# Top-32 attention and a squared-ReLU FFN on one core: the late loop's scores, mark passes and dense pieces in another order, and the pairing of four more steps on GpSimd

## Chip, cores and metric

One core of a Trainium2 chip runs the whole kernel. The metric is the device time of one execution in microseconds (us), the median of several runs. The engines are TensorE (PE), VectorE (DVE), ScalarE (ACT), GpSimd (POOL) and SyncE (SP), which issues most of the transfers. Each works through its own queue in order and waits where an operand or a buffer is not ready.

## What is computed

Eight batches of eight heads, 576 positions, head size 64. Each row of scores keeps its 32 largest values; their softmax weighs v. The eight heads of a position side by side give x (4608 x 512), which goes through a dense layer with a squared ReLU.

```python
scores = scale * np.matmul(q, k.transpose(0, 1, 3, 2))
kth = np.partition(scores, -top_k, axis=-1)[..., -top_k:-top_k + 1]
scores = np.where(scores >= kth, scores, -1000000000.0)
attn = np.exp(scores - np.max(scores, axis=-1, keepdims=True))
attn = attn / (np.sum(attn, axis=-1, keepdims=True) + 1e-09)
x = np.matmul(attn, v)                     # then (4608, 512)
h = np.maximum(x @ w_in, 0.0)              # 512 -> 2048
return h * h @ w_out                       # 2048 -> 512
```

## The kernel before

**Steps.** The attention is cut into 144 steps, numbered 0 to 143 (`U = 144`). A step holds two tiles of 128 rows by 576 scores. Steps 0 to 124 run in the first loop (L702), steps 125 (`Z = U - 19`) to 141 in the **late loop** (L798), the last two behind it. The change lies in the late loop and in `split`, which both loops use. All operations are pinned: each engine works in the order in which the program writes them.

**The life of a step u**, spread over several turns of the loop:

- `ahead` calls `scores` (L206): PE multiplies q and k (L213) into two PSUM tiles, `sc_b` for the second half of the columns and `sc_a` for the first, and ACT copies them into a buffer `s` in SBUF (L219, first `sc_b`, then `sc_a`). There is one `sc_a` and one `sc_b` for all steps. In turn u of the late loop this is done for step u + 3.
- `split` (L237, for step u + 2) and `join` (L260) pair the columns off: `cat` gets the pairwise maxima and minima of the two halves, and again of the halves of these. `split` has two forms. In the **old form** DVE does three operations of 128 x 288 (L253, L254, L256). In the **lent form** DVE does one maximum of 128 x 576 (L251), and the minima come from GpSimd: `mins` (L272) adds the two halves (L278), and `catch_up` (L267), a turn later, subtracts the maxima from the sum (L270). In the lent form the far half of the maxima lies in SBUF, and `bring` (L232) has PE move it, by a product with the identity (L235), into a free part of `sc_b` called `far`, where `join` reads it. `bring(u + 2)` comes behind the copy of `sc_b` for step u + 3, since both use that bank. Where a step is also **joint**, the minima of `join` go to GpSimd as well (a larger addition and one more subtraction), and `join` is one DVE operation (L263) instead of two.
- `topk` (L292) searches the 32 largest in four rounds on DVE: two MAX8 (L302) and, but for the last round, two MATCH_REPLACE8 (L306) each. ACT makes a small tile `low` from the maximum (L345).
- `below` (L352) is a **mark pass**: ACT marks the scores under the 32nd largest of one tile (L354), so two per step. `expo` (L361) is ACT's exponential of both tiles (L363), `mask` (L357) GpSimd's addition that takes the marked weights out (L359), `turn` (L400) a transposing transfer on SP's queue (L402), `products` (L683) PE's products of weights and v (L429), `invert` DVE's reciprocal of the sums (L434), and `place` (L449) ACT's scaled copies of the result into `x_tok` (L457).

**Dense pieces.** Once x of 128 tokens is complete, SP transposes it and the FFN's work on it is put into two lists. An **up piece** is eight products by w_in (L531) into one of two PSUM tiles named `gen`; later ACT takes the ReLU (L537) into a buffer `rl`, and the square follows on GpSimd (L545) or on ACT (L542). A **down piece** is four products by w_out (L559); every fourth is followed by an output copy on ACT (L566) and a store. `piece` (L582) first calls `flush`, which writes what ACT still owes for earlier pieces, and then takes one up or down piece in turn; `idle_piece` (L575) fills PE with products nobody reads.

**The planner.** `owe` adds up estimated work for GpSimd and ACT in `debt`, which each turn lowers (L58). `split` lends if GpSimd's debt is low; the square goes to ACT where GpSimd's debt is high and ACT's is not (L540). A change in one place can thus move a square in another.

**One turn of the late loop** before the change, shortened to the lines that matter here:

```python
below(u - 1, 0)
below(u - 1, 1)
...
split(u + 2)
topk(u, (0,))
...
mins(u + 2)
weights(u - 1)      # mask and turn
...
ahead(u + 3)
topk(u, (1,))
piece()
bring(u + 2)
products(u - 2)
topk(u, (2, 3))
join(u + 2)
...
expo(u)
```

Behind these stand `place(u - 2)` and two or three more pieces (L850).

Of the kernel before, what the change touches and what calls it, by code (L numbers as in the profile page):

```python
# [22 lines left out]
def kernel(  # L23
# [22 lines left out]
    def pin(ins):  # L46
        tc.keep_in_program_order(ins)
        return ins

    debt = {"G": 0.0, "A": 0.0}  # L50

    def owe(**more):
        for e, t in more.items():
            debt[e] += t
# [3 lines left out]
    def pass_step(more=0.0):  # L58
        for e in debt:
            debt[e] = max(0.0, debt[e] - {"G": 5.76, "A": 6.0}[e] - more)  # L60
# [134 lines left out]
    U = len(steps)  # L195
    Z, DEEP = U - 19, 9
# [39 lines left out]

    def split(u):  # L237
        d = st[u]
        lend = (2 < u < U - 20 and debt["G"] < 4.9) or Z < u < U - 5
        d["joint"] = lend and DEEP + 5 <= u < U - 6 and debt["G"] < (4.9 if u < Z + 2 else 5.5) - 1.22  # L240
        if d["joint"]:
            owe(G=1.36)
        cat = d["cat"] = scp.tile([128, 2, S], f32, name="cat", bufs=3)
        tops = d["tops"]
        one, two = sc[0][:, :, 0:HALF], d["s"][:, :, 1, :]
        tt = nc.vector.tensor_tensor
        if lend:
            owe(G=1.22)
            d["lent"] = True
            quarters = [z.rearrange("p x (j n) -> p x j n", j=2) for z in (one, two)]  # L250
            pin(tt(tops, *quarters, op=ALU.max))  # L251
        else:
            pin(tt(far, one[:, :, QUAR:HALF], two[:, :, QUAR:HALF], op=ALU.max))  # L253
            pin(tt(tops[:, :, 0, :], one[:, :, 0:QUAR], two[:, :, 0:QUAR], op=ALU.max))  # L254
        if not lend:
            pin(tt(cat[:, :, HALF + QUAR:S], one[:, :, QUAR:HALF], two[:, :, QUAR:HALF], op=ALU.min))  # L256
        if "rest" in d:
            d.pop("rest")()
# [75 lines left out]
    def sums_checked(by, lo, hi):  # L334
        pin(by.tensor_scalar(flags[:, 2, lo:hi], shares[:, lo:hi], scalar1=2.0 ** -12, scalar2=0.0, op0=ALU.is_ge, op1=ALU.is_equal))
# [13 lines left out]
    def pairwise(z):  # L349
        return z.rearrange("p (j n) -> p j n", j=2)  # L350

    def below(u, x):  # L352
        d = st[u]
        pin(nc.scalar.activation(pairwise(marks[u % 2][:, x, :]), d["s"][:, x], AF.Relu, bias=d["m"][3][:, x, 7:8], scale=-1.0))  # L354
        follow()
# [17 lines left out]
    def follow():  # L373
        while later:
            later.pop(0)()
# [7 lines left out]
    def flush():  # L383
        while late:
            late.pop(0)()
# [196 lines left out]
    def piece():  # L582
        flush()
        turn_of[0] ^= 1
        for q_ in ((ups, downs), (downs, ups))[turn_of[0]]:
            if q_:
                q_.pop(0)()
                return True
        return False
# [90 lines left out]
    def ok(w):  # L680
        return 0 <= w < U

    def products(w):  # L683
        if ok(w):
            for x in range(2):
                weigh(w, x)
# [8 lines left out]
    def ahead(w):  # L695
        if w < U:
            for i, c, a in steps[w]:
                while coming <= i or (coming == i + 1 and soon):
                    prepare(u)
            scores(w)  # L700
# [89 lines left out]
    def weights(w):  # L790
        mask(w)
        turn(w)

    def move():
        while moves:
            moves.pop(0)(u)

    for u in range(Z, U - 2):  # L798
        now[0] = u
        pass_step(0.3)  # L800
        owe(A=3.86, G=2.92)
        below(u - 1, 0)
        below(u - 1, 1)
        move()
        split(u + 2)
        topk(u, (0,))
        if u == Z:
            products(u - 3)
            invert_two(u - 4)
            place(u - 5)  # L810
            place(u - 4)
        if checks:
            note()
        mins(u + 2)
        if u == U - 8:
            sums_checked(nc.gpsimd, 0, OLD)
        weights(u - 1)
        square()
        hold["squares"] = False
        for go in ripe.pop(u, ()):  # L820
            go()
        ahead(u + 3)
        topk(u, (1,))
        if not piece():
            idle_piece()
        bring(u + 2)
        products(u - 2)
        if u < U - 4:
            topk(u, (2, 3))
        else:  # L830
            topk(u, (2,), lambda: invert(u - 2))
            topk(u, (3,))
        join(u + 2)
        if u == Z:
            invert(u - 3)
        if u < U - 4:
            invert(u - 2)
        if u == U - 4:
            piece()
        flush()  # L840
        expo(u)
        flush()
        if u == Z:
            place(u - 3)
        place(u - 2)
        turn_x(u)
        hold["squares"] = True
        for _ in range(2 if u == U - 19 else 1):
            prepare(u)
        for n in range(3 if u >= U - 12 and u != U - 4 else 2):  # L850
            if not piece() and n == 0:
                idle_piece()

# [10 lines left out]
    u = U - 2  # L864
# [72 lines left out]
    u = U - 1  # L937
# [190 lines left out]
```

## Time and profile before

| | |
|---|---|
| median of 3 runs | 842.77 us (842.25 to 844.38) |
| the profiled execution's own time | 843.64 us |
| its span, first to last recorded instruction | 841.8 us |
| mean granted clock of TensorE, share of full speed | 0.994 |
| instructions | 19913 |

The page of the profile lists for each engine its busy time and share of the span. A timeline lists one engine's instructions with start and duration in us; instructions that follow each other overlap a little, so what one costs its queue is read from start to start. The number in square brackets is idle time ahead of an instruction, with what ended it. The waits add such idle time up by what waited and what released it, and the chain of waits is followed back from the last instruction. All times of the trace count from the start of the span. Turn 125 of the late loop starts near 714 us on ACT, and one turn there takes about 6 us.

### The profile page before, as it was taken

What the parts mean: (1) busy time and instruction counts of PE and PEld (TensorE: products, weight loads), DVE (VectorE), ACT (ScalarE), POOL (GpSimd) and SP (SyncE); (2) the same over time, 40 slices, a digit from 0 to 9 for tenths busy, and PEclk for the clock granted to TensorE, in tenths of its full rate; (3) what the DMA queues carried; (4) which work ended last, traced back from release to release, by engine and by line L of the source; (5) the groups of instructions that cost most, each with busy time, mean ns of one, the idle gap of its engine ahead of it and who ended that gap; (6) DMA issues with size and microseconds to landing.
All of it is one profiled execution on the core that took longest, in us unless ns stands there. A gap on an engine that the chain in (4) does not pass through costs nothing.

```text
span 841.8 us, 19913 instructions
## 1 busy us (share of the span) xinstructions
PE 710.4 (84%) x6061; PEld 446.6 (53%) x6062; DVE 816.4 (97%) x3411; ACT 791.5 (94%) x1513; POOL 785.0 (93%) x638
## 2 busy tenths in 40 slices
PE   8898987788888879788788888788888888989986
PEld 4554545455545545455555554455555554656554
DVE  5999999999999999999999999999999999999995
ACT  4897999999999999999999999999999999999983
POOL 3788999999999999999999999999999999999771
PEclk9999999999999999999999999999999999999999
DMA  4796786654546556445565455555566557433442
GB/s 112 163 216 158 193 178 112 111 118 101 118 105 104 117 111 130 97 103 109 114 124 110 104 111 124 124 111 109 118 104 124 118 104 152 79 76 64 94 84 55
DMA packets 300883, 98.06 MB, mean 116 GB/s; under 512 B 284768, under 2 KB 293216, under 8 KB 300768
## 3 DMA queue, kind: packets, MB, share of 16 engines
q1 hardware_dynamic: 299424, 96.28, 56.1%
q8 instruction: 50, 0.82, 0.4%
q14 instruction: 65, 0.53, 0.2%
q10 hardware_dynamic: 1344, 0.43, 0.2%
HBM read 36.70 MB, written 9.44 MB: 55 GB/s over the span
## 4 chain that ended last, share of the span: by engine, by line
DVE 53%; issue 15%; POOL 13%; ACT 11%; PE 7%; DVEq 0%; ACTq 0%; POOLq 0%
DVE m L302 23%; DVE cat L306 15%; DVE s L251 7%; POOL cat L270 7%; DVE cat L263 5%; POOL cat L278 5%; ACT s L219 3%; ACT h L542 2%; PE sc_b L235 2%; ACT rl L537 1%; ACT marks_b L354 1%; ACT marks_a L354 1%; ACT w_two_a L363 1%; PE sc_b L213 1%; PE dn_ps L578 1%
## 5 line engine op out<-in xcount | busy, mean ns | idle before, releaser
L302 DVE MAX8 m<-cat 128x8 f32<-128x100 f32 (+3 forms) x1152 | 428.7, 414 | 0.2
L278 POOL TENSOR_TENSOR cat<-s 128x864 int32<-128x864 int32 (+2 forms) x144 | 265.0, 1840 | 5.9 <-DVE cat L263 3.5
L306 DVE MATCH_REPLACE8 cat<-m,cat 128x100 f32<-128x100 f32 (+2 forms) x864 | 252.7, 300 | 0.1
L270 POOL TENSOR_TENSOR cat<-cat,s 128x576 int32<-128x576 int32 (+1 forms) x144 | 196.3, 1363 | 3.3 <-DVE s L251 1.8
L213 PE MATMUL sc_b<-qkT 64*128 64x288 f32 (+1 forms) x640 | 117.4, 447 | 55.3 <-DVE cat L263 49.2
L235 PE MATMUL sc_b<-s,id_f 128*128 128x144 f32 x536 | 98.3, 306 | 57.4 <-ACT s L219 56.5
L559 PE MATMUL dn_ps<-w_out,h 128*128 128x512 bf16 x560 | 143.9, 382 | 1.3 <-POOL h L545 0.7
L531 PE MATMUL gen<-xT,w_in 128*128 128x256 bf16 (+1 forms) x1088 | 128.6, 263 | 1.9 <-ACT rl L537 1.1
L235 PEld LDWEIGHTS sc_b<-s,id_f 128*128 128x128 f32 x536 | 75.0, 190 | 101.0 <-ACT s L219 97.4
L531 PEld LDWEIGHTS <-w_in 128*128 128x128 bf16 x1344 | 110.2, 98 | 32.3 <-issue 19.7
L354 ACT ACTIVATE marks_a<-s,m 128x576 bf16<-128x576 f32 x144 | 124.2, 871 | 0.4 <-POOL w_two_c L359 0.2
L354 ACT ACTIVATE marks_b<-s,m 128x576 bf16<-128x576 f32 x142 | 118.5, 847 | 0.0
L219 ACT ACTIVATE s<-sc_b 128x576 f32<-128x576 f32 x144 | 103.7, 720 | 15.5 <-PE sc_b L213 8.2
L213 PE MATMUL sc_a<-qkT 64*128 64x288 f32 (+1 forms) x640 | 111.5, 430 | 0.4 <-DVE s L251 0.3
L219 ACT ACTIVATE s<-sc_a 128x576 f32<-128x576 f32 x144 | 104.8, 728 | 5.5 <-PE sc_a L213 3.7
L251 DVE TENSOR_TENSOR s<-sc_a,s 128x576 f32<-128x576 f32 x134 | 100.2, 748 | 0.0
L537 ACT ACTIVATE rl<-gen 128x512 f32<-128x512 f32 x140 | 96.3, 692 | 0.5 <-PE gen L531 0.5
L213 PEld LDWEIGHTS sc_b<-qkT 64*128 64x128 f32 (+1 forms) x640 | 47.6, 175 | 85.5 <-DVE cat L263 64.9
L270 POOL TENSOR_TENSOR cat<-cat 128x288 int32<-128x288 int32 x113 | 89.2, 789 | 0.9 <-DVE shares L434 0.9
L542 ACT ACTIVATE h<-rl 128x512 bf16<-128x512 f32 x123 | 89.2, 729 | 0.0
L559 PEld LDWEIGHTS <-h 128*128 128x128 bf16 x560 | 47.8, 98 | 68.4 <-issue 31.9
L263 DVE TENSOR_TENSOR cat<-sc_b,s 128x288 f32<-128x288 f32 x175 | 75.0, 444 | 5.8 <-PE sc_b L235 5.8
(137 smaller groups left out, 1190.5 us busy)
## 6 DMA issues: line engine op xcount, KB each, us to landing
v_raw<-in_v_dram SPq DMA_DIRECT2D x31, 256.0 KB, 3.1
out_dram<-wide SPq DMA_DIRECT2D x31, 256.0 KB, 2.9
q_raw<-in_q_dram SPq DMA_DIRECT2D x30, 256.0 KB, 3.6
k_raw<-in_k_dram SPq DMA_DIRECT2D x30, 256.0 KB, 3.6
h<-in_moe_w_in_dram SPq DMA_DIRECT2D x8, 512.0 KB, 5.1
h<-in_moe_w_out_dram SPq DMA_DIRECT2D x8, 512.0 KB, 4.7
q_raw<-in_q_dram SPq DMA_DIRECT2D x32, 32.0 KB, 3.1
v_raw<-in_v_dram SPq DMA_DIRECT2D x32, 32.0 KB, 2.7
```

What stands on the lines that cost most here:

```text
L213: pin(nc.tensor.matmul(out=sc[j][r if rest else slice(0, 128), x, 0:HALF], lhsT=qkT[r, 0, c * 128:min(S, (c + 1) * 128)], rhs=qkT[r, 1, j ...
L219: pin(nc.scalar.activation(s[:, :, j, :], sc[j][:, :, 0:HALF], AF.Copy))
L235: pin(nc.tensor.matmul(out=far[:, x, :], lhsT=id_f[:, :], rhs=st[w]["tops"][:, x, 1, :], start=True, stop=True))
L251: pin(tt(tops, *quarters, op=ALU.max))
L263: pin(nc.vector.tensor_tensor(d["cat"][:, :, lo:lo + QUAR], far, d["tops"][:, :, 0, :], op=op))
L270: pin(nc.gpsimd.tensor_tensor(at, at, top, op=ALU.subtract))
L278: pin(nc.gpsimd.tensor_tensor(cat[:, :, QUAR + lo:QUAR + hi], both[:, :, 0, lo:hi], both[:, :, 1, lo:hi], op=ALU.add))
L302: pin(nc.vector.max(out=m[r][:, x, :], in_=cat[:, x, at]))
L306: pin(nc.vector.match_replace(out=cat[:, x, at], in_to_replace=m[r][:, x, :], in_values=cat[:, x, at], imm_value=NEG))
L354: pin(nc.scalar.activation(pairwise(marks[u % 2][:, x, :]), d["s"][:, x], AF.Relu, bias=d["m"][3][:, x, 7:8], scale=-1.0))
L531: pin(nc.tensor.matmul(out=hp[:, n * n_rows:(n + 1) * n_rows], lhsT=w_in[:, kh, (f0 + n) * 128:(f0 + n + 1) * 128], rhs=xt(kh), start=(kh ...
L559: pin(nc.tensor.matmul(out=op[:, :], lhsT=held["h2"][:, f, c * 128:(c + 1) * 128], rhs=w_out[:, f, :], start=(f == 0), stop=(f == NF - 1)))
```

## The change

Four edits, in two functions:

1. `split` lends under another condition. Steps 124, 125, 139 and 140 now take the lent form (124 and 125 are also joint); before they took the old one.
2. The second mark pass and `move` (transposes of x that PE does) stand behind `ahead(u + 3)` instead of ahead of `split`.
3. `ahead(u + 3)` stands ahead of `weights`, `square` and the pieces that come ripe, instead of behind them. With edit 2 ACT's two copies of scores lie between the two mark passes.
4. One dense piece is done behind `products(u - 2)`, and one fewer at the end of the turn.

```diff
--- before.py
+++ after.py
@@ -236,7 +236,7 @@
 
     def split(u):
         d = st[u]
-        lend = (2 < u < U - 20 and debt["G"] < 4.9) or Z < u < U - 5
+        lend = 2 < u < U - 3 and (debt["G"] < 4.9 or u > Z)
         d["joint"] = lend and DEEP + 5 <= u < U - 6 and debt["G"] < (4.9 if u < Z + 2 else 5.5) - 1.22
         if d["joint"]:
             owe(G=1.36)
@@ -800,8 +800,6 @@
         pass_step(0.3)
         owe(A=3.86, G=2.92)
         below(u - 1, 0)
-        below(u - 1, 1)
-        move()
         split(u + 2)
         topk(u, (0,))
         if u == Z:
@@ -814,17 +812,20 @@
         mins(u + 2)
         if u == U - 8:
             sums_checked(nc.gpsimd, 0, OLD)
+        ahead(u + 3)
+        below(u - 1, 1)
+        move()
         weights(u - 1)
         square()
         hold["squares"] = False
         for go in ripe.pop(u, ()):
             go()
-        ahead(u + 3)
         topk(u, (1,))
         if not piece():
             idle_piece()
         bring(u + 2)
         products(u - 2)
+        piece()
         if u < U - 4:
             topk(u, (2, 3))
         else:
@@ -847,7 +848,7 @@
         hold["squares"] = True
         for _ in range(2 if u == U - 19 else 1):
             prepare(u)
-        for n in range(3 if u >= U - 12 and u != U - 4 else 2):
+        for n in range(2 if u >= U - 12 and u != U - 4 else 1):
             if not piece() and n == 0:
                 idle_piece()
```

ScalarE's queue in a turn of the middle of the late loop, before: `marks_a` is what the mark passes write, `s` the copied scores, `rl` the ReLU of an up piece, `gen` its PSUM tile, `h2` its square, `x_tok` the placed result.

```order
L354 ACTIVATE marks_a_117<-s_9643,m_9874 128x576
L219 ACTIVATE s_9981<-sc_b_123 128x2x288
L219 ACTIVATE s_9981<-sc_a_122 128x2x288
L345 ACTIVATE low_9990<-neg_9988 128x1
L537 ACTIVATE rl_9992<-gen_9948 128x512
L537 ACTIVATE rl_10023<-gen_9994 128x512
L363 ACTIVATE w_two_b_104<-s_9715,low_9990 128x2x576
L542 ACTIVATE h2_9901<-rl_9992 128x512
L542 ACTIVATE h2_9901<-rl_10023 128x512
L457 ACTIVATE x_tok_9091<-av_ps_121,shares_120 128x64 x2
L537 ACTIVATE rl_10040<-gen_10031 128x512
L354 ACTIVATE marks_b_118<-s_9715,m_9874 128x576 x2
```

And with the change, the same turn:

```order
L354 ACTIVATE marks_a_117<-s_9640,m_9873 128x576
L219 ACTIVATE s_9977<-sc_b_123 128x2x288
L219 ACTIVATE s_9977<-sc_a_122 128x2x288
L354 ACTIVATE marks_a_117<-s_9640,m_9873 128x576
L345 ACTIVATE low_9990<-neg_9988 128x1
L537 ACTIVATE rl_9992<-gen_9949 128x512
L537 ACTIVATE rl_10015<-gen_9994 128x512
L537 ACTIVATE rl_10034<-gen_10017 128x512
L363 ACTIVATE w_two_b_104<-s_9714,low_9990 128x2x576
L542 ACTIVATE h2_9901<-rl_9992 128x512
L542 ACTIVATE h2_9901<-rl_10015 128x512
L457 ACTIVATE x_tok_9091<-av_ps_121,shares_120 128x64 x2
```

The first mark pass is still ahead of the two copies and the second one is behind them; three ReLUs stand ahead of the exponential, where there were two and a third one behind the placing.

GpSimd's queue where step 124 is split (`cat_9563`) and then step 125 (`cat_9635` before, `cat_9634` with the change), before:

```order
L278 TENSOR_TENSOR cat_9563<-s_9482 128x2x144
L545 TENSOR_TENSOR h2_9097<-rl_9605 128x512
L359 TENSOR_TENSOR w_two_b_104<-w_two_b_104,marks_b_118 128x2x288
L163 CAST vau_a_97<-v_raw_115 128x10x64
L270 TENSOR_TENSOR cat_9563<-cat_9563,s_9482 128x2x144
L278 TENSOR_TENSOR cat_9635<-s_9571 128x2x144
L359 TENSOR_TENSOR w_two_c_105<-w_two_c_105,marks_a_117 128x2x288
```

And with the change:

```order
L278 TENSOR_TENSOR cat_9563<-s_9482 128x2x432
L359 TENSOR_TENSOR w_two_b_104<-w_two_b_104,marks_b_118 128x2x288
L163 CAST vau_a_97<-v_raw_115 128x10x64
L270 TENSOR_TENSOR cat_9563<-cat_9563 128x2x144
L270 TENSOR_TENSOR cat_9563<-cat_9563,s_9482 128x2x288
L278 TENSOR_TENSOR cat_9634<-s_9569 128x2x432
L359 TENSOR_TENSOR w_two_c_105<-w_two_c_105,marks_a_117 128x2x288
```

The additions (L278) of these steps grow from 128 x 2 x 144 to 128 x 2 x 432, the subtraction (L270) of step 124 becomes two, and the square (L545) has left GpSimd's queue for ACT's.

## Rows read from the trace of the kernel before

**Rows 1.** The page, first part: busy us (share of the span) and instructions of each engine.

```profile
PE 710.4 (84%) x6061; PEld 446.6 (53%) x6062; DVE 816.4 (97%) x3411; ACT 791.5 (94%) x1513; POOL 785.0 (93%) x638
```

**Rows 2.** Busy time by stretch: window, length, busy (instructions) per engine, PEclk, DMA share, GB/s.

```profile
760.00:780.00 20.00, 19.62 (x212) 13.78 (x212) 18.50 (x82) 20.00 (x43) 18.90 (x15) 1.00 0.48 80
800.00:820.00 20.00, 16.62 (x183) 10.67 (x180) 19.87 (x87) 16.67 (x33) 14.71 (x15) 1.00 0.40 81
```

**Rows 3.** The waits from 700 to 842 us: waiter, releaser, total us, count, median.

```profile
DVE cat L263 <- PE sc_b L235: 4.0, 6, 1.1
```

**Rows 4.** The chain of waits from 690 to 842 us: start, us, instruction.

```profile
732.92 0.55 ACT s L219
733.51 0.77 PE sc_b L235 x4
734.38 0.46 DVE cat L263
```

**Rows 5.** ScalarE in order of time, 717 to 736: start, us, instruction [idle before <-releaser].

```profile
717.88 0.93 ACT L457 ACTIVATE x_tok<-av_ps,shares 128x64 bf16<-128x64 f32 x4 [0.21 <-DVE shares L434]
...
731.36 1.56 ACT L354 ACTIVATE marks_b<-s,m 128x576 bf16<-128x576 f32 x2
732.69 0.77 ACT L219 ACTIVATE s<-sc_b 128x576 f32<-128x576 f32 x1
733.22 0.78 ACT L219 ACTIVATE s<-sc_a 128x576 f32<-128x576 f32 x1
733.75 0.34 ACT L345 ACTIVATE low<-neg 128x1 f32<-128x1 f32 x1
733.85 1.23 ACT L537 ACTIVATE rl<-gen 128x512 f32<-128x512 f32 x2
734.80 1.41 ACT L363 ACTIVATE w_two_c<-s,low 128x1152 bf16<-128x1152 f32 x1
```

**Rows 6.** VectorE in order of time, 700 to 708 us.

```profile
700.06 0.47 DVE L253 TENSOR_TENSOR sc_b<-sc_a,s 128x288 f32<-128x288 f32 x1
...
701.16 0.42 DVE L302 MAX8 m<-cat 128x8 f32<-128x100 f32 x2
...
705.68 0.81 DVE L263 TENSOR_TENSOR cat<-sc_b,s 128x288 f32<-128x288 f32 x2
706.40 0.75 DVE L251 TENSOR_TENSOR s<-sc_a,s 128x576 f32<-128x576 f32 x1
707.06 0.42 DVE L302 MAX8 m<-cat 128x8 f32<-128x100 f32 x2
```

**Rows 7.** GpSimd in order of time, 698 to 718 us.

```profile
698.44 0.78 POOL L270 TENSOR_TENSOR cat<-cat 128x288 int32<-128x288 int32 x1
699.19 1.40 POOL L270 TENSOR_TENSOR cat<-cat,s 128x576 int32<-128x576 int32 x1
700.56 0.79 POOL L278 TENSOR_TENSOR cat<-s 128x288 int32<-128x288 int32 x1
701.32 1.03 POOL L545 TENSOR_TENSOR h<-rl 128x512 bf16<-128x512 f32 x1
...
706.14 1.41 POOL L359 TENSOR_TENSOR w_two_c<-w_two_c,marks_a 128x576 int32<-128x576 int32 x1 [0.25 <-ACT w_two_c L363]
...
708.25 2.02 POOL L278 TENSOR_TENSOR cat<-s 128x864 int32<-128x864 int32 x1
711.16 1.42 POOL L359 TENSOR_TENSOR w_two_a<-w_two_a,marks_b 128x576 int32<-128x576 int32 x1 [0.88 <-ACT w_two_a L363]
...
716.62 1.42 POOL L359 TENSOR_TENSOR w_two_b<-w_two_b,marks_a 128x576 int32<-128x576 int32 x1
```

**Rows 8.** TensorE in order of time, 721 to 736 us.

```profile
721.96 0.48 PE L429 MATMUL av_ps<-vau_c,wT 128*128 128x65 bf16 x10 [0.22 <-DMA wT<-w_two_b]
...
734.11 0.47 PE L429 MATMUL av_ps<-vau_e,wT 128*128 128x65 bf16 x10
734.63 1.03 PE L531 MATMUL gen<-xT,w_in 128*128 128x256 bf16 x8
```

## The prediction

> **What bounds the kernel now.** I read five views in this order. The busy line of the page [rows 1] has VectorE (DVE) at 97%, with ScalarE (ACT), GpSimd (POOL) and TensorE (PE) not far below; it cannot tell which of them holds up the late loop, where the change lies. The busy time by stretch [rows 2] can: from 760 to 780 us ACT is busy all 20.00 us and DVE only 18.50, while from 800 to 820 DVE has 19.87 and ACT 16.67. So ACT bounds the first part of the late loop and DVE its end. The waits [rows 3] name what DVE misses: six times, 4.0 us in all, `join` (L263) waits for PE's `bring` (L235). The chain of waits [rows 4] shows where that comes from: an ACT copy of scores (L219), then `bring`, then `join`; `bring(u+2)` may not begin before ACT has read the bank of `scores(u+3)`. ACT's own instructions in order of time [rows 5] leave no hole: two mark passes 1.33 us (0.67 each), each copy 0.53, the small `low` 0.10, each relu 0.48, then the exponential, each beginning where the one before leaves off. While this lasts, every microsecond that ACT loses or gains is one of the kernel.
>
> **DVE's work.** In steps 124, 125, 139 and 140 three DVE operations become one. From the start of the split to the next operation it is 1.10 us in the old form and 0.66 in the new [rows 6]: 0.44 saved, four times. In 124 and 125 `join` also drops from two operations to one, 0.36 each (half of the 0.72 between its start and the next row). Sum 4 x 0.44 + 2 x 0.36 = 2.5 us. I credit nothing for it: two steps lie just ahead of the stretch in which DVE waits for ACT anyway, and two in the tail, where ACT will by then be the late one. If that cover were gone, 2.5 us is what they bring. PE gets four more `bring`s at about 0.6 us and one idle piece, beside DVE's work.
>
> **The copies sooner.** ACT does the same operations per step in another order. Moving one mark pass behind the copies brings them 0.67 us forward; one square that the planner takes from GpSimd adds about 0.5 us to ACT (an estimate: as much as a relu of the same 128x512, 0.48), and it stands ahead of all late copies. Net 0.2 us sooner: on a saturated queue the new place alone yields next to nothing. I add as much again for one wait that ACT need not repeat: -0.4 us.
>
> **GpSimd.** Steps 124 and 125 each get a longer addition (2.02 instead of 0.79 us), a longer subtraction (1.40 instead of 0.78, which one of the short shape 128x288 takes) and a new subtraction for the joint half (0.78 too), all from [rows 7]; one square of 1.03 us leaves. That is 2 x (1.23 + 0.62 + 0.78) - 1.03 = +4.2 us. The two idle gaps there (0.25 and 0.88) swallow 1.1, so GpSimd is 3.1 us late from its 711 us on, on a queue that has no further gap for a long while. What hangs on it is the masking of the weights: SP transposes them, PE multiplies, DVE inverts the sums, ACT places the result. SP's queue gains no transfer; its output stores and token transposes stand behind a later transpose, and none of them is needed within the step.
>
> From the start of a masking to the products that wait for it the rows have 5.34 us (716.62 to 721.96) [rows 7, 8]. The masking of step 123 then begins at 711.16 + 3.1 = 714.3, its products at 719.6, and with 0.5 us of products DVE inverts at about 720.1, where it did so just ahead of ACT's placing at 717.88 [rows 5]. ACT's second pair of placings stood at 718.28 (717.88 plus half of the four's time) and now at 719.9 to 720.3: **1.6 us lost** to 2.0; I take the lower, since 5.34 is the slowest of such transposes near there. DVE's split behind the inversion, and so the next scores, come late too: **0.3 us**. One step later the masking of step 124 begins at 719.7, its products at 725.1. Behind these the new order puts a second dense piece, whose relu ACT has to do ahead of the exponential: 725.1 + 0.5 + 1.03 = 726.6, and ACT would stand there at 723.9 (a copy at 721.6 plus the 2.3 us worked out next): up to 2.7, taken as **2.5 us**.
>
> **The second piece: a wait that was not there.** Before, PE did this piece at the end of the step and ACT its relu after the exponential, which covered it. Now PE does it after `bring` and the products, and ACT wants its relu before the exponential. PE's way from the start of a copy: 0.82 to `bring` (732.69 to 733.51), 0.60 to the products, 0.52 to the piece, 1.03 for the piece [rows 4, 5, 8]: 2.97 us. ACT's way from the same copy: two copies and `low` 1.16, the second mark pass 0.67, one relu 0.48: 2.31. ACT waits 0.66 us. With one more relu between (2.79) the gap would be 0.2, but then there are three relus in a row and two banks named `gen`: the third piece may not start before the first relu has read its bank (1.83 + 0.75, one relu of [rows 5] being 1.23 - 0.48), and ends at 3.6: a wait of 0.8. Where an output copy (128x512 like a relu) lies between, or the second piece is a down piece, it is nothing. By the order, the second piece is an up piece in twelve of the steps 126 to 139; eleven come after step 126, so **11 x 0.66 = 7.3 us**. The bounds are 0.2 each (2.2) and, with nothing in between and the bank not free, 0.75 + 1.03 - 0.48 = 1.3 each (14). I stay near the middle, since steps of each kind alternate.
>
> **The sum.** 1.6 + 0.3 + 2.5 + 7.3 - 0.4 = 11.3 us on ACT. ACT has 3.3 us of idle time from 800 to 820 [rows 2], in which it can catch up; I take off 2.5. Left: **+8.8 us**. The profiled execution took 843.6 us (span 841.8), so 852.4; it lies 0.9 above the median 842.8 of the runs, against which the forecast is **851.6 us**.
>
> **A rule against the row.** The stretches of [rows 2] say that ACT bounds the place of the change. The Trainium skill, Perfetto Trace Analysis, section Identifying the Most-Contended Engine, says to take the engine with the highest occupancy as the bottleneck, which over the span is DVE; by it the change would attack the right engine, and the sum would be the first rival's. The same page notes that kernels can have several regimes, and the stretches here show two.
>
> **The rivals.**
> - *DVE is the bound, and faster.* If ACT could absorb the piece, DVE would lose its 4.0 us of waits [rows 3] and 2.5 us of work: 842.8 - 6.5 = 836.3 us. It decides at the copy: it has to end a whole `bring` before DVE ends its search, in steps where ACT is filled. For it: the copies do stand earlier in the queue. Against it: the queue has no holes [rows 5], and the new order puts waits into it.
> - *GpSimd's lateness alone.* The pieces are ready in time, but the weights stay 3.1 us late through the stretch: 3.1 less 0.9 for the two late splits, 845.0 us. For it: GpSimd has no gap. Against it: the first lateness already holds a piece back.
> - *Nothing to be seen.* The relus are covered because ACT is still behind PE, and only 1.6 + 0.3 of the start remain, less 0.9 and 0.4: 843.4 us. For it: before the change PE was never what ACT's relus missed here. Against it: PE's way of 2.97 us starts at ACT's own copy, so ACT being behind delays both.
> - That the change does not do what it says is excluded by the order: the new form of split stands in all four steps.
>
> **How the numbers follow.** The forecast has 0.72 and by itself reaches from 847.5 (0.3 to 0.4 per piece) to 855.0 (about 0.9 per piece). GpSimd alone 0.08, nothing 0.11, faster 0.09. Within 0.3% (2.5 us, about what a measurement of this kernel can tell from no change) lie the two middle rivals, so same 0.19; faster 0.09; slower 0.72. The range for 8 in 10 takes in the two middle rivals and reaches 842.0 to 855.0; left out are the faster rival and the ends.
>
> **What would show it.** Right: a few waits of ACT at the relu (L537) for PE's up piece (L531), near 0.7 us each and 7 us in all; one wait of ACT's placing (L457) for DVE's inversion near 719; GpSimd's masking of step 123 near 714; DVE waiting more, not less, at `join`. Wrong: ACT's queue as full as before with no waits at relus, and DVE's waits at `join` gone; then the piece was covered, and the time lies at the rivals.

## The result, and the profile after

The changed kernel takes **853.30 us** (median of four runs, 850.22 to 853.72), the kernel before 843.11 in the same comparison: a ratio of 1.0107, 95% interval 1.0093 to 1.0121, or **9.0 us slower** (7.8 to 10.2; the medians lie 10.2 apart). The profiled execution took 853.72 us, with a span of 851.9. The forecast was 851.6, 8.8 us slower, with a range from 842.0 to 855.0.

The first part of the page, to be held against [rows 1]:

```profile
PE 709.9 (83%) x5999; PEld 451.0 (53%) x6082; DVE 814.5 (96%) x3401; ACT 792.6 (93%) x1514; POOL 791.5 (93%) x639
```

PE, DVE and ACT are as busy as before, within 2 us; GpSimd has 6.5 us more. ACT does 792.6 us of work instead of 791.5. So the time went into waits, and the page's busy line does not show where.

The busy time by stretch does (columns as in [rows 2]):

```profile
760.00:780.00 20.00, 18.61 (x170) 11.94 (x172) 17.24 (x74) 18.48 (x38) 16.00 (x13) 0.94 0.33 76
800.00:820.00 20.00, 17.75 (x161) 10.93 (x165) 18.98 (x81) 17.89 (x37) 18.29 (x18) 1.00 0.43 83
```

From 760 to 780 us ACT, which had no idle time at all before, has 1.5 us, and DVE 2.8 instead of 1.5; the granted clock is 0.94 where it was 1.00. From 800 to 820 the stretch lies earlier in the program than before, since all is late by then.

The waits from 690 us on (waiter, releaser, total us, count, longest; the last number in [rows 3] is the longest too, not the median):

```profile
DVE cat L263 <- PE sc_b L235: 12.3, 13, 1.7
...
ACT rl L537 <- PE gen L531: 6.6, 10, 1.1
```

DVE's waits at `join` have tripled (4.0 us in six before, [rows 3]), and ACT waits 6.6 us at ReLUs for the piece that PE has not done yet. One of these ten waits, 0.5 us near the end of the span, stands in the kernel before as well.

GpSimd in order of time, for [rows 7]:

```profile
697.64 0.78 POOL L270 TENSOR_TENSOR cat<-cat 128x288 int32<-128x288 int32 x1
...
699.76 2.01 POOL L278 TENSOR_TENSOR cat<-s 128x864 int32<-128x864 int32 x1
...
713.32 1.40 POOL L359 TENSOR_TENSOR w_two_a<-w_two_a,marks_b 128x576 int32<-128x576 int32 x1
```

The subtraction that stood at 698.44 is here at 697.64, so this execution came to the place 0.80 us sooner. The masking of step 123 (`w_two_a`, `marks_b`), 711.16 before, is at 713.32: 2.16 us late, or 2.96 with the 0.80. The forecast had 3.1. The addition of step 124 (699.76) takes 2.01 us, where the short one took 0.79, and the square that followed it has gone.

ACT in order of time, for [rows 5], from the end of turn 125 to turn 127 (idle time before an instruction, and its releaser, in brackets):

```profile
719.30 0.93 ACT L457 ACTIVATE x_tok<-av_ps,shares 128x64 bf16<-128x64 f32 x4 [1.34 <-PE gen L154]
...
722.47 0.65 ACT L219 ACTIVATE s<-sc_b 128x576 f32<-128x576 f32 x1 [1.41 <-PE sc_b L213]
723.43 0.65 ACT L219 ACTIVATE s<-sc_a 128x576 f32<-128x576 f32 x1 [0.31 <-PE sc_a L213]
...
725.11 0.60 ACT L537 ACTIVATE rl<-gen 128x512 f32<-128x512 f32 x1 [0.28 <-PE gen L531]
726.78 0.60 ACT L537 ACTIVATE rl<-gen 128x512 f32<-128x512 f32 x1 [1.07 <-PE gen L531]
...
732.34 1.10 ACT L537 ACTIVATE rl<-gen 128x512 f32<-128x512 f32 x2
734.13 0.60 ACT L537 ACTIVATE rl<-gen 128x512 f32<-128x512 f32 x1 [0.69 <-PE gen L531]
```

PE in order of time, for [rows 8]:

```profile
715.22 0.65 PE L235 MATMUL sc_b<-s,id_f 128*128 128x144 f32 x4
718.20 0.73 PE L429 MATMUL av_ps<-vau_b,wT 128*128 128x65 bf16 x10 [2.33 <-DMA wT<-w_two_a]
...
719.27 1.89 PE L578 MATMUL dn_ps<-fill,id_h 128*128 128x512 bf16 x4
721.09 1.33 PE L213 MATMUL sc_b<-qkT 64*128 64x288 f32 x4
...
723.31 1.76 PE L531 MATMUL gen<-xT,w_in 128*128 128x256 bf16 x8
...
733.00 1.91 PE L531 MATMUL gen<-xT,w_in 128*128 128x256 bf16 x16 [0.72 <-ACT rl L537]
```

Two things are to be seen. In turn 127 ACT does two ReLUs (732.34), waits 0.69 us, and does the third (734.13): PE could begin that piece only at 733.00, after 0.72 us with nothing else to do, because both tiles `gen` were full until ACT had read one. And in turn 125 PE waits 2.33 us for the transposed weights; behind that wait everything on PE is slow: the four score products of `sc_b` take 1.33 us (0.76 in the trace of before, at 719.03), the idle products 1.89 (1.04 there, at 716.82), the up piece 1.76 (1.03 in [rows 8]). The same products in the trace of before:

```profile
716.82 1.04 PE L578 MATMUL dn_ps<-fill,id_h 128*128 128x512 bf16 x4
719.03 0.76 PE L213 MATMUL sc_b<-qkT 64*128 64x288 f32 x4 [1.18 <-ACT qkT L157]
```

The granted clock of the same stretch (window, length, PE busy, PEclk, DMA share, GB/s):

```profile
714.00:716.00 2.00, 1.82 (x11) 1.00 0.02 4
716.00:718.00 2.00, 0.00 (x0) 1.00 1.10 212
718.00:720.00 2.00, 1.80 (x14) 0.50 0.11 22
...
724.00:726.00 2.00, 2.00 (x23) 0.80 0.21 32
```

PE ran at the upper level (2.4 GHz, 1.00), was idle from 715.9 to 718.2, and from then until a little behind 724 had the lower one (1.2 GHz, 0.50). A second fall lies further on: the granted clock is 0.89 from 755 to 760 us and 0.76 from 760 to 765. The profile of before has no fall between 320 and 835 us. Ahead of that it has two, in the 5 us from 70 and in the 5 us from 315 (0.66 each), and the changed kernel has two there as well.

### The profile page after: what moved, and what is told of

Its sections match the earlier page's. It is cut to its first block, busy times and chain, and to the rows that moved or that the text cites. A ratio compares the mean times of both kernels' runs of the same rounds, so it can differ in the third digit from the quotient of the medians.

```text
span 851.9 us, 19859 instructions
## 1 busy us (share of the span) xinstructions
PE 709.9 (83%) x5999; PEld 451.0 (53%) x6082; DVE 814.5 (96%) x3401; ACT 792.6 (93%) x1514; POOL 791.5 (93%) x639
## 4 chain that ended last, share of the span: by engine, by line
DVE 47%; issue 16%; POOL 13%; PE 12%; ACT 10%; DMA 2%; SPq 0%; ACTq 0%; DVEq 0%; POOLq 0%
DVE m L302 21%; DVE cat L306 14%; POOL cat L270 7%; DVE s L251 7%; POOL cat L278 5%; DVE cat L263 5%; ACT s L219 2%; PE gen L531 2%; PE sc_b L213 2%; PE sc_b L235 2%; ACT marks_a L354 1%; PE dn_ps L578 1%; DMA wT<-w_two_a 1%; ACT h L542 1%; PE dn_ps L559 1%
## 5 line engine op out<-in xcount | busy, mean ns | idle before, releaser
L278 POOL TENSOR_TENSOR cat<-s 128x864 int32<-128x864 int32 (+2 forms) x144 | 268.8, 1867 | 5.5 <-DVE cat L263 3.1
L270 POOL TENSOR_TENSOR cat<-cat,s 128x576 int32<-128x576 int32 (+1 forms) x144 | 198.9, 1381 | 2.4 <-DVE s L251 0.9
L235 PE MATMUL sc_b<-s,id_f 128*128 128x144 f32 x552 | 101.2, 306 | 58.0 <-ACT s L219 56.9
L559 PE MATMUL dn_ps<-w_out,h 128*128 128x512 bf16 x492 | 133.1, 384 | 8.0 <-issue 4.2
L235 PEld LDWEIGHTS sc_b<-s,id_f 128*128 128x128 f32 x552 | 77.3, 190 | 102.4 <-ACT s L219 98.4
L219 ACT ACTIVATE s<-sc_b 128x576 f32<-128x576 f32 x144 | 100.3, 696 | 17.3 <-PE sc_b L213 10.6
L219 ACT ACTIVATE s<-sc_a 128x576 f32<-128x576 f32 x144 | 101.2, 703 | 5.7 <-PE sc_a L213 3.3
L251 DVE TENSOR_TENSOR s<-sc_a,s 128x576 f32<-128x576 f32 x138 | 102.8, 745 | 0.0
L537 ACT ACTIVATE rl<-gen 128x512 f32<-128x512 f32 x140 | 90.3, 649 | 6.7 <-PE gen L531 6.6
L270 POOL TENSOR_TENSOR cat<-cat 128x288 int32<-128x288 int32 x115 | 91.1, 792 | 0.0
L542 ACT ACTIVATE h<-rl 128x512 bf16<-128x512 f32 x124 | 84.6, 689 | 0.0
```

The source lines that it names most:

```text
L219: pin(nc.scalar.activation(s[:, :, j, :], sc[j][:, :, 0:HALF], AF.Copy))
L235: pin(nc.tensor.matmul(out=far[:, x, :], lhsT=id_f[:, :], rhs=st[w]["tops"][:, x, 1, :], start=True, stop=True))
L270: pin(nc.gpsimd.tensor_tensor(at, at, top, op=ALU.subtract))
L278: pin(nc.gpsimd.tensor_tensor(cat[:, :, QUAR + lo:QUAR + hi], both[:, :, 0, lo:hi], both[:, :, 1, lo:hi], op=ALU.add))
L559: pin(nc.tensor.matmul(out=op[:, :], lhsT=held["h2"][:, f, c * 128:(c + 1) * 128], rhs=w_out[:, f, :], start=(f == 0), stop=(f == NF - 1)))
```

## Experiments

All runs are compared with the kernel before on the same chip; the ratio is given with its 95% interval, and what it makes of 843.1 us.

| kernel | edits | us | ratio | interval |
|---|---|---|---|---|
| the change | 1, 2, 3, 4 | +9.0 | 1.0107 | 1.0093 to 1.0121 |
| lend_only | 1 | +2.6 | 1.0031 | 1.0021 to 1.0041 |
| order_only | 2, 3 | +0.3 | 1.0003 | 0.9993 to 1.0014 |
| piece_only | 4 | +11.4 | 1.0135 | 1.0115 to 1.0155 |
| lend_order | 1, 2, 3 | +2.6 | 1.0031 | 1.0019 to 1.0043 |
| order_piece | 2, 3, 4 | +8.4 | 1.0100 | 1.0083 to 1.0117 |
| relu_behind | all, ReLU moved | +5.4 | 1.0064 | 1.0047 to 1.0081 |
| lend_head_only | 1 for 124, 125 | +4.7 | 1.0056 | 1.0040 to 1.0073 |
| head_not_joint | 1 for 124, 125, not joint | +1.1 | 1.0013 | 1.0003 to 1.0022 |
| order_tail | 2, 3, 1 for 139, 140 | +2.1 | 1.0025 | 1.0012 to 1.0039 |
| after_fill | all, PE filled | +9.7 | 1.0115 | 1.0099 to 1.0130 |
| order_fill | 2, 3, tail filled | +0.2 | 1.0002 | 0.9991 to 1.0013 |
| order_down_fill | 2, 3, 4 for down pieces, tail filled | +4.2 | 1.0050 | 1.0036 to 1.0065 |

### The change taken apart

**Edit 1 alone:**

```diff
-        lend = (2 < u < U - 20 and debt["G"] < 4.9) or Z < u < U - 5
+        lend = 2 < u < U - 3 and (debt["G"] < 4.9 or u > Z)
```

> The kernel before with edit 1 alone (steps 124, 125, 139, 140 lent). Three theories of the +10.2 us. Piece theory (mine): about 6 us come from ACT's waits at the ReLU of the second piece, about 4 from the start; here no piece is moved, so only GpSimd's lateness shows: 3.1 us late at the masking of step 123, placing 1.6 us late, +1 to +3 us. GpSimd theory: the longer pairings of 124 and 125 set everything behind them late: +7 to +10. Clock theory: nearly all of it is the granted clock falling while PE waits for weights: +3 to +6, with a fall of the clock near 720, and otherwise nothing.

Measured +2.6, inside the piece theory's range; the GpSimd theory's +7 to +10 is out. The clock theory's +3 to +6 is not excluded by the number (the interval makes 1.8 to 3.5 us), and the granted clock does fall in this trace (0.66 from 720 to 725 us). The trace of edits 1 to 3, below, tells the two apart.

**Edits 2 and 3 alone** (the second `below` and `move` behind `ahead(u + 3)`, that ahead of `weights`):

```diff
         below(u - 1, 0)
-        below(u - 1, 1)
-        move()
...
         mins(u + 2)
...
+        ahead(u + 3)
+        below(u - 1, 1)
+        move()
         weights(u - 1)
...
-        ahead(u + 3)
         topk(u, (1,))
```

> The kernel before with edits 2 and 3 alone (copies between the mark passes, scores ahead of the weights). Piece theory: -1 to 0 us, since ACT's queue holds the same work and the copies are 0.67 us sooner. GpSimd theory: 0. Clock theory: 0, no fall of the clock before 800. If DVE is what counts, its waits at join (4.0 us before) go down and it is up to 4 us faster.

Measured +0.3, and its interval takes in 1.0000. DVE's waits at `join` fell to 2.0 us in three, but the time did not follow: ACT's work stayed the same (791.4 us). Against the expectation this trace has a fall of the clock before 800 us, at 700; more on it below.

**Edit 4 alone:**

```diff
         products(u - 2)
+        piece()
...
-        for n in range(3 if u >= U - 12 and u != U - 4 else 2):
+        for n in range(2 if u >= U - 12 and u != U - 4 else 1):
```

> The kernel before with edit 4 alone (a piece behind the products, one fewer at the end of the turn). Piece theory: the waits of ACT at the ReLU (L537) appear, and each is longer than in the change, because no mark pass lies between the copies and the ReLUs: PE's way of 2.97 us against ACT's 1.64 is up to 1.3 us in a turn, +6 to +13 us. GpSimd theory: 0 to +1. Clock theory: 0 to +2.

Measured +11.4. The waits in its trace (waiter, releaser, total us, count, longest):

```profile
DVE cat L263 <- PE sc_b L235: 12.6, 9, 2.0
...
ACT rl L537 <- PE gen L531: 9.9, 11, 1.6
```

ACT waits 9.9 us at the ReLU, in 11 waits of 0.9 on average (one of them is the 0.5 us near the end that the kernel before has too): longer than the 0.7 of the change, as expected without a mark pass between.

**Edits 1 to 3, without 4:**

> The change without its edit 4 (the pieces stand where they stood before). Piece theory: the ReLU waits are gone and only the start is left: +1 to +4 us. GpSimd theory: still +7 to +10. Clock theory: +3 to +6 with a fall of the clock near 720.

Measured +2.6. The waits of its trace:

```profile
DVE cat L263 <- PE sc_b L235: 3.6, 6, 1.0
...
ACT rl L537 <- PE gen L531: 0.5, 1, 0.5
```

The ReLU waits have gone (one of 0.5, as in the kernel before), and with them 6.4 of the 9.0 us. Edit 4 accounts for that much in the change; the other edits soften it from the 11.4 it costs by itself.

This trace also shows the late weights without the slow clock. GpSimd's masking of step 123 starts at 713.21, as late as in the change. PE and ACT in order of time, and the window (length, PE busy, PEclk, DMA share, GB/s):

```profile
718.20 0.48 PE L429 MATMUL av_ps<-vau_b,wT 128*128 128x65 bf16 x10 [2.41 <-DMA wT<-w_two_a]
...
720.20 0.76 PE L213 MATMUL sc_b<-qkT 64*128 64x288 f32 x4 [0.28 <-ACT qkT L157]
```

```profile
721.00 0.65 ACT L219 ACTIVATE s<-sc_b 128x576 f32<-128x576 f32 x1 [0.19 <-PE sc_b L213]
```

```profile
720.00:725.00 5.00, 4.22 (x41) 1.00 0.62 144
```

PE waits as long for the weights (2.41 us, 2.33 in the change), but no fall of the clock follows, the scores take 0.76 us, and ACT waits 0.19 us for them where in the change it waits 1.41 and 0.31. So about 1.5 us of what the change loses in turn 126 is the slow clock. The late weights delay ACT without it too: this trace goes from 1.1 us ahead of the trace of before, at the exponential of step 121, to 1.5 behind it at that of step 126.

**Edits 2 to 4, without 1:**

> The change without its edit 1 (old condition for lending). Piece theory: the parts add up, so the change's +9.0 less the 2.6 that edit 1 costs alone: +5 to +8 us, with eight or more waits of ACT at the ReLU (L537). GpSimd theory: 0 to +2, since its queue is as before. If the lateness of edit 1 and the piece feed each other (a late GpSimd queue makes the piece late), it is under +5.

Measured +8.4, a little over the range; the ReLUs wait 6.2 us in nine there. Edit 1 (2.6) and the rest (8.4) make 11.0, and together they cost 9.0: what is late already by GpSimd need not be late for the piece as well. That last reading is an argument, not a measurement.

### Why edit 1 costs at the start

Steps 124 and 125 alone (the first pair of lines), and then the same steps lent but not joint (both pairs):

```diff
-        lend = (2 < u < U - 20 and debt["G"] < 4.9) or Z < u < U - 5
+        lend = (2 < u < U - 18 and debt["G"] < 4.9) or Z < u < U - 5
...
-        d["joint"] = lend and DEEP + 5 <= u < U - 6 and debt["G"] < (4.9 if u < Z + 2 else 5.5) - 1.22
+        d["joint"] = lend and DEEP + 5 <= u < U - 6 and u not in (Z - 1, Z) and debt["G"] < (4.9 if u < Z + 2 else 5.5) - 1.22
```

> The kernel before with edit 1 for steps 124 and 125 alone. If the start's 4 us of lateness come from GpSimd's longer queue there, this has the whole loss of edit 1: +3 to +4.5 us, with the fall of the granted clock near 720. If the two steps at the end (139, 140) cost as well, it is under +2.6.

> The kernel before with steps 124 and 125 in the lent form but not joint: DVE does the two operations of join as before, GpSimd has 1.2 us less in each of the two steps. If GpSimd's lateness is what edit 1 costs at the start (the kernel with these two steps lent and joint lost 5.0 us), the loss nearly goes: -0.5 to +1.5 us, and GpSimd's masking of step 123 starts under 1 us later than before. If DVE's or PE's part of the lending costs (the bring, scores behind it), it stays at +3 to +5.

Measured +4.7, a little over its range, and +1.1, inside it. GpSimd's masking of step 123 in order of time, first lent and joint, then lent alone:

```profile
714.55 1.39 POOL L359 TENSOR_TENSOR w_two_a<-w_two_a,marks_b 128x576 int32<-128x576 int32 x1
```

```profile
711.89 1.41 POOL L359 TENSOR_TENSOR w_two_a<-w_two_a,marks_b 128x576 int32<-128x576 int32 x1 [0.18 <-ACT w_two_a L363]
```

Before it started at 711.16 [rows 7]. The first is 3.4 us late, the second 0.7 (of which ACT's exponential of step 120, at 694 us, had 0.4 and 0.2 already), and the time follows. The bring and the shorter split stand in both kernels, so it is GpSimd's queue that costs: the joint half is what it had no room for. The square that leaves GpSimd for ACT does so in both kernels, and the exponential of step 122 loses 0.5 us by it in both traces. The clock is a part of the difference: it fell near 720 in the first trace (0.66 from 720 to 725 us) and not in the second. But from the exponential of step 121 to that of step 126 the first trace loses 3.3 us, and that of edits 1 to 3, as late and without a fall there, 2.6; so the fall is the smaller part.

The two steps at the end stay open. Edit 1 with them costs 2.1 us less than without (+2.6 against +4.7), but edits 2 and 3 with them (`Z < u < U - 3` as the second half of the condition) cost 1.8 more than without:

> Edits 2 and 3, and edit 1 for steps 139 and 140 alone: the parts of the change that lost nothing by themselves. If edit 1 costs only by 124 and 125 and the two steps at the end save DVE 0.44 us each: -2 to 0 us. If the end's steps cost too: +1 to +2.

Measured +2.1; -2 to 0 was expected if edit 1 costs at 124 and 125 only, and +1 to +2 if the two steps cost as well. Of the difference to order_only 1.44 us stand in the trace before step 139 is split: ACT's exponential of step 136 is that much later (783.73 and 782.29), with the same instructions up to there. Another 1.5 come between the exponentials of steps 139 and 140. There the transposing transfer of step 138's weights took 5.0 us from issue to landing, where it took 3.4 in order_only; PE waited 1.83 us for it, and ACT 2.18 for the down piece behind that. Nothing shows that the two steps made this transfer slow. The other pair of traces points the other way: from the exponential of step 138 to that of step 140 lend_only gains 0.8 us on the kernel before, and lend_head_only loses 0.1. What the two steps do at the end is not shown.

### Is it ACT's wait, or PE's order?

The second piece stays where it is on PE, but its ReLU goes behind the exponential on ACT:

```diff
-        flush()
         expo(u)
         flush()
```

> The change with one line less: no flush ahead of the exponential, so that the ReLU of the second piece comes behind it on ACT, while PE does the piece where the change has it. Piece theory, with ACT's wait as its mechanism: the ReLU waits go, and the time is that of edits 1 to 3 alone, +2 to +4 us. If it is PE's order that costs (the piece delays the scores behind it), it stays at +7 to +10.

Measured +5.4, between the two. Of edit 4's 6.4 us 3.6 went. The waits of its trace:

```profile
POOL h L545 <- ACT rl L537: 3.8, 3, 1.7
...
ACT rl L537 <- PE gen L531: 1.4, 2, 0.9
```

ACT's waits at the ReLU fell from 6.6 to 1.4 us (0.5 of them the wait near the end), but GpSimd, which is as full as ACT, now waits 3.8 us (0.9 in the change) for ReLUs that come later, and its squares stand ahead of other work there. A wait was moved to another full queue. That this makes all of the 2.8 us that are left over edits 1 to 3 alone is not shown: ACT also waits 2.7 us in six for scores, which stand behind the piece on PE (1.1 of it in turn 126, where the clock had fallen).

The piece theory had an assumption in it that a down piece costs nothing. Here edit 4 is done for down pieces only. This kernel and the one it is compared with (order_fill, edits 2 and 3) also have six idle products in the tail, told of below:

```diff
         products(u - 2)
+        done = 0
+        if downs:
+            flush()
+            downs.pop(0)()
+            done = 1
...
-        for n in range(3 if u >= U - 12 and u != U - 4 else 2):
+        for n in range((3 if u >= U - 12 and u != U - 4 else 2) - done):
```

> As the kernel before it in this call (edits 2 and 3, filled tail), with edit 4 for down pieces alone: behind the products only a down piece, where there is one, and one piece fewer at the end of that turn. Piece theory: a down piece needs no ReLU, so no waits of ACT at L537 of over 0.5 us: within 1.5 us of the kernel before it. If a second piece costs by its place on PE, whatever it is: +4 us or more over it.

Measured +4.2 against before, and 4.0 over order_fill. The piece theory's expectation (within 1.5 us) failed, and the other one's (+4 or more) came. ACT's waits from 720 us on:

```profile
ACT s L219 <- PE sc_b L213: 4.1, 6, 1.0
...
ACT wide L566 <- PE dn_ps L559: 2.8, 4, 0.8
...
ACT rl L537 <- PE gen L531: 0.9, 2, 0.6
```

The ReLUs hardly wait any more (0.6 of the 0.9 us is the wait near the end), but every fourth down piece ends in an output copy that ACT has to make ahead of the exponential, and that waits just as a ReLU does (2.8 us in four, 0.2 in one in order_fill). And the scores, which stand behind the piece on PE, come late (4.1 in six; 1.2 in two in order_fill). So it is not the kind of piece: with a second piece in the middle of the turn, PE's result and PE's next scores are not there yet when ACT asks for them.

### The granted clock

Can PE be kept busy in turn 125, and what is the fall of the clock worth?

```diff
         bring(u + 2)
+        if u == Z:
+            idle_piece(8, "gen", 2)
         products(u - 2)
```

> The change with eight idle products on PE in turn 125, in the 2.33 us in which PE waits for the transposed weights. If the fall of the granted clock behind that wait (0.52 from 720 to 725) costs the 2 to 3 us by which the change's start jumps beyond the forecast: +6 to +7 against before instead of +9.0, no fall of the clock near 720, and a start that is some 2 us less late at step 126. If the fall costs nothing because the wait itself does: +9 as before, or more by what the filling delays the products.

Measured +9.7, and not what was expected of it: the idle products ran (715.72 to 717.6), then PE still waited 1.79 us for the weights, and the products began 1.2 us later than in the change (the transfer of the weights took 4.6 us from issue to landing, 3.4 there; why is not shown), and the clock fell all the same (windows as above, all engines, PEclk third from the end):

```profile
715.00:720.00 5.00, 3.16 (x25) 1.83 (x24) 2.82 (x10) 2.96 (x6) 5.00 (x4) 1.00 0.81 95
720.00:725.00 5.00, 4.72 (x22) 2.46 (x22) 5.00 (x24) 3.81 (x10) 5.00 (x6) 0.66 0.62 144
```

This run does not price the clock. Other traces do, besides that of edits 1 to 3 above. The tail first, with six idle products ahead of the products of step 141:

```diff
-    def empty(bank, times=1):
-        for n in range(times):
+    def empty(bank, times=1, first=0):
+        for n in range(first, times):
...
     x_last((0,))
+    empty(two, 4, 1)
     products(u - 2)
```

> Edits 2 and 3 alone, with six idle products on PE ahead of the products of step 141, where the run of edits 2 and 3 had 1.59 us of waiting for the transposed weights and a granted clock of 0.50 right behind it. That run had its exponential of turn 141 start 1.38 us sooner than before and ended 0.2 later. If the clock took it: -1.0 to -1.5 us against before, the clock whole from 820 to 832. If the transfer of the weights takes it whatever the clock: -0.3 to +0.5.

Measured +0.2, which is what was expected if the transfer of the weights takes the time whatever the clock (-0.3 to +0.5). PE in order of time at the end of order_only:

```profile
822.62 0.48 PE L429 MATMUL av_ps<-vau_f,wT 128*128 128x65 bf16 x10 [1.59 <-DMA wT<-w_two_a]
822.94 0.72 PE L917 MATMUL sc_a<-xT,w_in 128*128 128x128 bf16 x8
823.46 1.06 PE L917 MATMUL sc_b<-xT,w_in 128*128 128x128 bf16 x8
824.31 1.91 PE L559 MATMUL dn_ps<-w_out,h 128*128 128x512 bf16 x4
```

And of order_fill:

```profile
824.13 1.46 PE L859 MATMUL sc_b<-fill,w_two_a 128*128 128x512 bf16 x6
825.46 0.48 PE L429 MATMUL av_ps<-vau_f,wT 128*128 128x65 bf16 x10
825.78 0.61 PE L917 MATMUL sc_a<-xT,w_in 128*128 128x128 bf16 x8
```

In order_only PE waits 1.59 us, and then eight products take 1.06 us and four of 512 columns 1.91; filled, the wait and the fall are gone, and from ACT's exponential of step 142 to the end of the span it takes 23.7 us instead of 24.7. So in these two executions the wait and the fall together were worth 1 us. (The trace of before, with a wait of 0.92 us there and no fall, takes 23.1.) The medians don't show it, and the profiles say what may hide it. Up to step 141 the two kernels are the same instructions. Yet (order_only first, then order_fill; all engines, PEclk third from the end):

```profile
700.00:705.00 5.00, 5.00 (x24) 1.96 (x25) 5.00 (x24) 4.57 (x11) 4.83 (x6) 0.66 0.69 158
720.00:725.00 5.00, 4.97 (x49) 3.33 (x48) 5.00 (x23) 5.00 (x11) 5.00 (x6) 1.00 0.32 87
```

```profile
700.00:705.00 5.00, 4.60 (x32) 2.24 (x32) 4.90 (x26) 5.00 (x11) 5.00 (x6) 1.00 0.57 124
720.00:725.00 5.00, 5.00 (x40) 3.48 (x37) 4.40 (x17) 3.79 (x7) 5.00 (x5) 0.71 0.73 133
```

In one execution the clock fell at 700 us, behind waits of PE of 1.23 and 0.42 us, and in the other at 719.5, behind waits of 0.33 and 1.22. Each also had waits like these at the other's place (1.23 and 0.40; 0.54 and 0.89), and no fall there. The first fall delayed ACT's exponentials by 0.8 us, the second by 1.4.

## Why the prediction was right

**The bound.** Right: with the same work, ACT's new waits became the time, and DVE's waits at `join` grew to 12.3 us. The forecast named both. The Trainium skill, Perfetto Trace Analysis, section Identifying the Most-Contended Engine, would have had DVE as the engine to relieve, by its share of the span; edits 2 and 3 alone relieved it (waits at `join` 2.0 us instead of 4.0) and moved the time by 0.3 us, so here the stretch decides and not the span.

**DVE's work.** The join and the split of step 124, for [rows 6], in DVE's order of time:

```profile
703.96 0.44 DVE L263 TENSOR_TENSOR cat<-sc_b,s 128x288 f32<-128x288 f32 x1
704.32 0.75 DVE L251 TENSOR_TENSOR s<-sc_a,s 128x576 f32<-128x576 f32 x1
704.98 0.42 DVE L302 MAX8 m<-cat 128x8 f32<-128x100 f32 x2
```

The join takes 0.36 us to the next start and the split 0.66, as forecast, and nothing came of it at the start. At the end it may have, which is open (above).

**The copies sooner.** -0.4 us forecast; +0.3 measured, with an interval (-0.6 to +1.2) that takes in both.

**GpSimd.** Right in size and place: 3.1 us late forecast, 2.96 measured, and the kernel without the joint half shows it as the cause. The placing that hangs on it stands at 719.30 instead of 717.88, behind 1.34 us of waiting: 1.4 us late, or 2.2 with the 0.80, where 1.6 to 2.0 was forecast. (The profile names L154 on PE as what ended that wait, and not DVE's inversion, the sign that was forecast.) Edits 1 to 3 alone cost 2.6 us, where the steps that concern them (1.6 + 0.3 - 0.4) make 1.5. The trace of that kernel is 1.5 us late at turn 126, but it had been 1.1 ahead at step 121, so the start lost 2.6, about 1 us more than forecast. Another 2.7 come at turn 132, behind a fall of the clock between 755 and 760.

**Turn 126.** The size was right and half of the reason wrong. 2.5 us forecast; ACT waited 3.1 there. But only 1.35 of it (0.28 + 1.07) is the second piece, for which products near 725.1 were forecast and stood at 725.40. The other 1.7 (1.41 + 0.31) is ACT waiting for scores that PE made at half the clock; in the trace of edits 1 to 3, with the weights as late and the clock at 1.00, that wait is 0.19. By the rows of that trace a second piece would have ended near 724.8 (723.81, where the products end, and 1.03), and ACT would have stood there at 723.3: a wait of 1.5, by this estimate, and not 2.5. That PE's wait for the late weights would let the clock fall was not in the forecast at all, so that the size came out was luck.

**The second piece.** 11 waits of 0.66 us were forecast, 7.3 in all. ACT's waits from 728 us to the end:

```profile
ACT rl L537 <- PE gen L531: 5.3, 8, 1.1
```

Eight waits, 5.3 us. The last of them, 0.53 at 828.97, is the one near the end that the kernel before has too (0.53 at 817.95). That leaves seven waits and 4.7 us: the size was the one forecast (0.68 each), the count too large. The second piece is an up piece in eleven turns behind 126, as counted. But in turns 133, 135 and 137 an output copy lies between the ReLUs, and ACT does not wait; the prediction put that case at nothing and counted these turns all the same. In turn 139 two ReLUs follow each other without a wait. Part of the size is luck: the first two waits (0.69 each in turns 127 and 128) are the case of three ReLUs and two tiles `gen`, for which 0.8 was worked out. (The Trainium skill, Perfetto Trace Analysis, section Optimization Strategy, takes a gap that repeats on a full engine as a possible sign of too few buffers. The trace agrees for these two turns: PE stood 0.72 us in each until a tile `gen` was read. No run here has a third tile.) The remark that a down piece costs nothing was wrong, as the kernel with down pieces alone shows: the waits for output copies (1.2 us in two in the change, 0.2 in one before) belong to the same term. The forecast for the piece, turn 126 included and what is given back taken off, was 2.5 + 7.3 - 2.5 = 7.3 us; by difference of kernels it is 6.4.

**Given back.** 2.5 us were taken off for ACT's idle time at the end. ACT's exponentials were 11.85 us late at most (806.73 against 794.88), and the span ended 10.1 late: 1.8.

**The sum.** That it came within 0.2 us of the 9.0 is luck in part. The waits at ReLUs behind turn 126 were 2.6 us less than forecast, and the wait of the second piece in turn 126 itself about 1 us less. Against that stand the late weights, about 1 us more than forecast, and two falls of the clock that were not in the sum: about 1.5 us in turn 126, and about 1.5 at turn 132, where the exponential loses 2.3 us and only 0.7 of it is a wait at a ReLU.

**The rivals.** DVE as the bound is out: its waits grew. GpSimd alone is not enough: it gives edit 1's 2.6. "Nothing to be seen" fell with the ReLUs that were not covered.

How much of the 9.0 us is clock stays partly open. Of the four runs of the change the one with a mean granted clock of 0.999 took 850.22 us, those at 0.990 to 0.993 took 852.9 to 853.7; so some 3 us come and go with it, falls ahead of the late loop among them, and 7 to 8 are there without (850.2 less the median of before, 843.1, or less its fastest run, 842.25). Four runs are few for this.

## What to carry to other kernels

When work is moved to fill a gap on one engine, look for the instruction on the other engine that will consume it, and where that stands in its queue: a piece done earlier on PE was a loss since ACT's ReLU moved earlier with it, ahead of work that had been its cover. Before a full queue gets more work, count its gaps: the joint half, for which GpSimd had hardly any, cost 3.6 us (4.7 less 1.1), the lent half 1.1. None of the versions tried beats the kernel before.

## What was not expected

- The clock falls behind short waits of PE, but not behind each: there was a fall behind 2.33 us in the change and none behind 2.41 in the trace of edits 1 to 3. The same instructions, in two kernels that differ only in the tail, had the fall at 700 us in one execution and at 719.5 in another, and the place decides the price: 0.8 us where down pieces were slow, 1.4 where scores were. So a profile shows one of several places where it can fall; within ten runs of order_only the time went from 842.39 us at a mean clock of 0.997 to 845.62 at 0.992. The Trainium skill, TensorE: Matmul & The Clock Gate, section What's actually happening, says of the rise at the start of TensorE's work that its moment is not tied to the kernel's start and varies from run to run; these executions show the same of the fall.
- With a gap filled by idle products the clock stayed up in the tail, and in turn 125 it did not: there PE still waited 1.79 us behind them.
- A transposing transfer of weights lands 3.5 us after its issue in the median (order_tail), but one there took 5.0 and one of after_fill 4.6, and PE waited for it. Such a turn can pass for an effect of the edit.
